# Clearing memory on another engine, and two moved transfers, in a fused gated-recurrence and squared-ReLU kernel

## The chip, the cores and the metric

The kernel runs on one core of a Trainium2 chip. A core has a matrix engine (TensorE, PE in the profile), an engine for elementwise work (VectorE, DVE), one for activation functions and copies (ScalarE, ACT), a programmable one (GpSimd, POOL) and one that mostly issues transfers (SyncE, SP). Each runs its own list of instructions in order, and they signal each other with semaphores. Transfers between the large memory and the on-chip memory are asked for from the queue of SyncE, ScalarE or GpSimd and are carried out by 16 DMA engines.

The metric is the time of one execution on the device in microseconds. Three runs of the kernel before the change gave 706.3 us as the median, 705.64 at the least and 706.55 at the most.

## The reference

A gated linear recurrence per head, and a feed-forward layer on its output. The shapes are 4 sequences, 8 heads, 768 steps, 48 channels a head; 3072 tokens, model width 384, inner width 2048.

```python
mag = sqrt(a_re**2 + a_im**2)
scale = minimum(mag, 0.999) / (mag + 1e-6)
a_re_n, a_im_n = a_re * scale, a_im * scale
for t in range(S):                              # S_re, S_im: [B, H, D, D], zero at first
    new_re = ar * S_re - ai * S_im              # ar, ai: a_re_n, a_im_n at step t
    new_im = ar * S_im + ai * S_re
    S_re, S_im = new_re + outer(k[t], v[t]), new_im
    y[t] = q[t] @ S_re
x = y as [B*S, H*D]                             # 3072 x 384
h = maximum(x @ w_in, 0)
out = (h * h) @ w_out                           # 3072 x 384
```

## The kernel before

The sequence is cut into chunks of 128 steps, and two chunks (`GC = 2`, `b` = 0 or 1) form a group; there are 12 groups (`NGR`). For each group VectorE and ScalarE make the operands (the gates, their running products, the scaled queries and keys), TensorE makes the attention-like products, and the token tile `x` goes through the feed-forward layer on TensorE.

The two weight matrices arrive as 64-bit words. They are fetched in 16 blocks, and VectorE decodes each with five instructions. The words of a block of `w_in` come in two halves of the partitions, one asked for from SyncE and one from GpSimd:

```python
def decode(dst, words, j):                      # dst: 128 x 768 elements of a weight matrix
    ...
    nc.vector.tensor_scalar(out=head, in0=high, scalar1=3, scalar2=0x3FFFFFF8, ...)       # L585
    nc.vector.scalar_tensor_tensor(out=head, in0=high, scalar=-2 ** 30, in1=head, ...)    # L587
    nc.vector.tensor_scalar(out=rest, in0=head, scalar1=-2 ** 23, scalar2=None, ...)      # L589
    ...
    nc.vector.scalar_tensor_tensor(out=rest, in0=low..., scalar=2.0 ** -52, in1=rest, ...) # L592
    tt(dst, head.bitcast(F32), rest, ALU.add)                                             # L480
```

The line L480 is a helper, `tt`, through which nearly all two-input operations of VectorE go. Some tiles have parts that no later instruction writes, or that are read before they are first written in full. They are cleared once:

```python
def turn_mask(step):
    if step == 0:
        nc.scalar.activation(out=sums[:, 0:1], in_=tiny, func=AF.Abs_reciprocal_sqrt)     # L538
        return
    if step == 2:
        for t in ([t[:, :, :, :, C:W] for t in qk_of] + last + [t[:, DM:] for t in vt]
                  + kt + prod + states[0] + states[1]):
            nc.gpsimd.memset(t, 0.0)                                                      # L544
        return
    ...
```

These are 16 instructions. Their sizes per partition, in 4-byte elements, are 2 x 48 (`qk`), 2 x 1040 (`last`), 4 x 16 (`vt`), 2 x 512 (`kt`), 2 x 24 (`prod`) and 4 x 512 (`state`). VectorE itself clears a few small tiles while the pools are set up, `carry` (288 elements, then 96 set to one) among them.

The steps of the operands that the text speaks of:

```python
def squares():                                   # o.0: ScalarE, L698
    nc.scalar.activation(out=tiles["sq"], in_=r[:, A_RE:A_IM + 1], func=AF.Square)
def sum_of_squares():                            # o.3: VectorE, L711, waits for the squares
    ...
def limit(): ...                                 # o.8, o.9: ScalarE, two copies of z (L683)
def lessened(): ...
def grown_factor(): ...                          # o.10: ScalarE, L743
def gates():                                     # o.11: VectorE
    ...                                          #   L749 (reads both copies)
    tt(both_parts, both_parts, f...)             #   L480
    ...                                          #   L753 (reads the factor)
def grown_squared():                             # o.22
    nc.gpsimd.memset(begun, 0.0)                 #   GpSimd, L763
    nc.scalar.activation(...)                    #   ScalarE, L764, then L766 and L767
def grow():                                      # o.13: VectorE, the scan L771
    ...
def last_heads():                                # o.21: SyncE, six transfers last<-qk, L831
    ...
```

Everything is ordered by hand. A long string names the steps, and each engine takes its part of each step in this order. The letters that matter here: `o` a step of the operands, `l` and `i` the loads of a group's inputs (`raw`), `f` and `j` the two halves of a fetch of words, `W` a check by ScalarE that reads a block's words, `D` the decoding of a block, `v` the load of a group's values (`vt`), `a` and `b` the steps of its two chunks, `g` the gap fill, `F` and `H` the first product and its squared ReLU, `Z` and `R` the products and sums of the second matrix, `s` a store, `M` the step `turn_mask`. Its beginning, one stretch around the first gap fill, and its end:

```python
"l0.0 M0 f0 j0 l0.1 i0.1 f1 j1 M2 f2 j2 v0 o0.0 o0.3 o0.1 o0.4 o0.5 o0.7 o0.2 M1 o0.8 "
"D0 o0.9 o0.10 o0.6 o0.11 W0 W1 D1 o0.22 f3 v1 j3 o0.12 W2 o0.13 o0.15 o0.14 f4 j4 W3 "
...
"v2 a0.7 o1.15 o1.14 g0 l2 i2 o1.16 F0.0 o1.17 F0.1 H0.0 D5 ..."
...
"Q11.2 Q11.1 Q11.0 Q11.3 Z11.3 R11.2 Z11.4 R11.3 Z11.5 R11.4 Z11.6 R11.5 s11.0 R11.6 "
"s11.1"
```

The gap fill copies parts of the token tile `x` into its unused partitions, and the first product of a group waits for it:

```python
def load_values(gi):                             # v
    for b, n in enumerate(groups[gi]):
        nc.sync.dma_start(out=vt[gi % 2 * GC + b][:, 0:DM], in_=in_turn(vtok, n))         # L520
def fill_gaps(i):                                # g
    for hh in range(HH):
        nc.sync.dma_start(out=x[pads(hh), 0:NG], in_=x[rows(hh), NG])                     # L955
def store(i, b):                                 # s
    nc.sync.dma_start(out=in_turn(out, groups[i][b]), in_=out_of[i, b])                   # L1002
```

The output tile of chunk 1 of a group, 128 x 384, is completed in two halves of columns (`left` is 0 to 191, `right` 192 to 383; `MH` = 192, `DM` = 384):

```python
elif r == 4:
    tt(o[1][:, right], chain, o[1][:, right], ALU.add)       # R.4, VectorE
elif r == 5:
    tt(o[0][:, right], others[1], o[0][:, right], ALU.add)   # R.5, VectorE
else:
    nc.scalar.copy(out=o[1][:, left], in_=chain)             # R.6, ScalarE, L1062
```

After the last store every engine reads `count`, a number that tells whether the data were in the ranges that this path is made for; with these data they are, and a general path (not shown) is jumped over.

Of the kernel before, what the change touches and what calls it, by code (L numbers as in the profile page):

```python
# [425 lines left out]
def quotient_path(ctx, tc, feat, vtok, w_in, w_out, w1, w2, out, n_seq, count):  # L426

    nc = tc.nc
    N, _, D, _, NP, C = feat.shape
    DM, FF = w_in.shape  # L430
# [4 lines left out]
    NGR = N // GC  # L435
# [34 lines left out]
    def pads(hh):  # L470
# [3 lines left out]
    groups = [[(bp * GC + b) * NCH + c for b in range(GC)]  # L474
              for bp in range(n_seq // GC) for c in range(NCH)]
# [37 lines left out]
    def in_turn(rows_, n):  # L513


        return rows_[n * C:(n + 1) * C].rearrange("(n j) m -> j n m", j=L)
# [18 lines left out]
# [6 lines that stand above are left out]

            for t in ([t[:, :, :, :, C:W] for t in qk_of] + last + [t[:, DM:] for t in vt]
                      + kt + prod + states[0] + states[1]):
                nc.gpsimd.memset(t, 0.0)  # L544
            return
        nc.scalar.copy(out=mask.rearrange("p (j n) -> p n j", j=L),
                       in_=plain.rearrange("p (n j) -> p n j", j=L))
        turned = pm.tile([C, C], F32, tag="m", name="turned")
        nc.tensor.transpose(turned, mask, ident)
        nc.scalar.copy(out=mask.rearrange("p (j n) -> p n j", j=L),  # L550
                       in_=turned.rearrange("p (n j) -> p n j", j=L))
# [398 lines left out]
    KH, MH = NFB // 2, DM // 2  # L950
# [44 lines left out]
    out_of = {}  # L995
# [3 lines left out]
        nc.scalar.copy(out=out_of[i, b], in_=o_of[i, b])  # L999

    def store(i, b):
        nc.sync.dma_start(out=in_turn(out, groups[i][b]), in_=out_of[i, b])  # L1002

# [36 lines left out]
    def outputs(i, r):  # L1042
# [27 lines left out]


    FRONT = (
        "l0.0 M0 f0 j0 l0.1 i0.1 f1 j1 M2 f2 j2 v0 o0.0 o0.3 o0.1 o0.4 o0.5 o0.7 o0.2 M1 o0.8 "
        "D0 o0.9 o0.10 o0.6 o0.11 W0 W1 D1 o0.22 f3 v1 j3 o0.12 W2 o0.13 o0.15 o0.14 f4 j4 W3 "
        "l1 i1 o0.16 W4 o0.17 D2 o0.18 o1.6 o0.19 f5 j5 o0.20 o1.0 W5 a0.1 o1.3 o0.21 o1.1 D3 "
        "a0.2 a0.3 o1.4 o1.5 a0.4 a0.8 o1.2 o1.7 f6 j6 b0.0 a0.9 o1.8 b0.1 b0.2 b0.5 o1.9 b0.6 "
        "D4 b0.3 b0.7 a0.0 b0.4 o1.10 W6 b0.8 o1.11 f7 j7 a0.5 o1.12 o1.22 a0.6 b0.9 o1.13 W7 "
        "v2 a0.7 o1.15 o1.14 g0 l2 i2 o1.16 F0.0 o1.17 F0.1 H0.0 D5 o1.18 F0.2 H0.1 o2.6 o1.19 "
        "f8 F0.3 H0.2 F0.4 H0.3 o1.20 o2.0 F0.5 H0.4 W8 a1.1 o2.3 o1.21 D6 a1.2 a1.3 o2.1 a1.4 "
        "a1.8 o2.4 o2.2 F0.6 D7 f9 H0.5 o2.5 a1.0 H0.6 a1.9 F0.7 a1.5 W9 f10 o2.7 a1.6 b1.1 "  # L1080
        "a1.7 D8 b1.0 o2.10 o2.8 H0.7 b1.5 o2.9 f11 b1.6 D9 b1.2 b1.3 b1.7 T0.0 b1.4 g1 W10 "
# [53 lines left out]
        "Z10.4 b11.5 b11.6 R10.4 Z10.5 b11.7 g11 Z10.6 R10.5 s10.0 F11.0 R10.6 s10.1 F11.4 "  # L1135
        "H11.0 F11.1 H11.4 X11.0 K0 Y11.0 F11.5 K1 H11.1 F11.2 H11.5 X11.1 Y11.1 F11.6 H11.2 "
        "F11.3 H11.6 X11.2 K2 Y11.2 F11.7 H11.3 Z11.0 H11.7 X11.3 Y11.3 Z11.1 R11.0 Z11.2 R11.1 "
        "Q11.2 Q11.1 Q11.0 Q11.3 Z11.3 R11.2 Z11.4 R11.3 Z11.5 R11.4 Z11.6 R11.5 s11.0 R11.6 "
        "s11.1")


    number_of = {}
# [1 line left out]
    def ranges(step):  # L1144
# [32 lines left out]
        "Z": half_product,  # L1177
        "R": outputs,
        "s": store,
        "f": fetch,  # L1180
        "j": lambda i: fetch(i, True),
# [4 lines left out]
        "l": load_parts,  # L1186
        "v": load_values,
        "M": turn_mask,
        "K": ranges,
    }  # L1190
# [13 lines left out]
@with_exitstack  # L1204
def kernel(
    ctx: ExitStack,
    tc: tile.TileContext,
    feat: bass.AP,
    vtok: bass.AP,
    w_in: bass.AP,  # L1210
    w_out: bass.AP,
    out: bass.AP,
    n_seq: int,
):
    nc = tc.nc
    DM, FF = w_in.shape
    wts = ctx.enter_context(tc.tile_pool(name="wts", bufs=1))
    w1 = wts.tile([P, DM // P, FF], F32, name="w1")
    w2 = wts.tile([P, FF // P, DM], F32, name="w2")
    count = wts.tile([1, 1], I32, name="count")  # L1220
    quotient_path(tc, feat, vtok, w_in, w_out, w1, w2, out, n_seq, count)
    n_good = nc.values_load(count, min_val=0, max_val=P)
    with tc.If(n_good < P):
        decode_weights(tc, w_in, w_out, w1, w2, feat.shape[2])
        general_path(tc, feat, vtok, w1, w2, out, n_seq)
# [30 lines left out]
```

## Time and profile before

| | us |
|---|---|
| median of three runs | 706.3 |
| span of the profiled execution, first to last instruction | 704.7 |
| TensorE busy | 623.7 (89%) |
| VectorE busy | 528.5 (75%) |
| ScalarE busy | 386.6 (55%) |
| GpSimd busy | 46.3 (7%) |

The mean granted TensorE clock is 0.996 of full speed. The busy shares are averages over stages with different limits: the first 200 us hold the decoding of the weights and the first groups, the rest the steady run. In 0 to 200 us VectorE is busy for 176.1 us and TensorE for 129.5; in 200 to 660 us TensorE is busy for 456.8 us of 460. A line of the timeline reads: start, duration, engine, source line, operation, the tile written and the tile read, their sizes, and in brackets how long the engine stood idle before and what released it. SPq, ACTq and POOL with DMA_DIRECT2D are issues of transfers. A line of the waits reads: the waiting engine, line and tile, what it waited for, and the total, the number of times and the longest.

### The profile page before, as it was taken

Reading aid. Unit: us, or ns where it says so; the run is one execution under the profiler, and the core shown is the slowest. Engines: PE = TensorE matmul, PEld = TensorE weight load, DVE = VectorE, ACT = ScalarE, POOL = GpSimd, SP = SyncE. Lnnn points to the kernel's source line nnn. Section 1 sums busy time; section 2 is a strip of 40 time slices with the busy share of each in tenths; the row PEclk is TensorE's granted clock in tenths of the full one; section 3 lists DMA queues with packets and bytes.
Section 4 is the critical chain, followed back from the end, with each engine's and each line's share of the span. In section 5 each row is a group of like instructions: output and inputs, shape, how many; then the busy total and the mean of one; then the engine's idle time right before and its main releaser. Section 6 shows DMA issues by size and latency. Waiting matters only on the chain.

```text
span 704.7 us, 12547 instructions
## 1 busy us (share of the span) xinstructions
PE 623.7 (89%) x4955; PEld 548.1 (78%) x4955; DVE 528.5 (75%) x916; ACT 386.6 (55%) x684; POOL 46.3 (7%) x106
## 2 busy tenths in 40 slices
PE   0007689999889999999999999999999999999995
PEld 0005577776578898998999989989989989989895
DVE  4998999999699786896785885995985976872130
ACT  6647487754648547537457557366376475340330
POOL 8322200000000000000000000000000000000000
PEclk9999999999999999999999999999999999999999
DMA  8776434461333063062061051151240340110101
GB/s 198 163 132 113 105 74 143 152 108 38 68 75 62 7 93 72 2 124 40 29 113 23 29 113 24 47 98 22 68 84 14 84 74 8 29 23 2 29 1 28
DMA packets 44036, 47.75 MB, mean 68 GB/s; under 512 B 6016, under 2 KB 38976, under 8 KB 43968
## 3 DMA queue, kind: packets, MB, share of 16 engines
q1 hardware_dynamic: 41280, 41.30, 28.0%
q0 software_dynamic: 2336, 5.21, 3.7%
q8 instruction: 41, 0.67, 0.4%
q10 hardware_dynamic: 352, 0.34, 0.2%
q14 instruction: 27, 0.22, 0.1%
HBM read 36.18 MB, written 4.72 MB: 58 GB/s over the span
## 4 chain that ended last, share of the span: by engine, by line
PE 73%; DVE 13%; DMA 7%; SPq 3%; ACT 2%; issue 1%; DVEq 0%; ACTq 0%
PE h_ps L961 30%; PE o_ps L1038 26%; PE a_ps L872 6%; DMA raw<-in_feat_dram 3%; PE y L898 3%; PE y L864 3%; PE add L919 2%; DVE ab L480 2%; PE tp L879 2%; DVE qk L480 1%; DMA words<-in_moe_w_in_dram 1%; SPq L831 1%; DMA vt<-in_vtok_dram 1%; DVE pr L480 1%; DVE room L480 1%
## 5 line engine op out<-in xcount | busy, mean ns | idle before, releaser
L961 PE MATMUL h_ps<-x,w 128*128 128x256 f32 x1152 | 257.6, 384 | 7.1 <-DMA x<-x 7.0
L961 PEld LDWEIGHTS h_ps<-x,w 128*128 128x128 f32 x1152 | 220.3, 192 | 38.5 <-issue 6.2
L966 ACT ACTIVATE h<-h_ps 128x512 f32<-128x512 f32 x96 | 57.5, 599 | 104.4 <-PE h_ps L961 96.0
L1038 PE MATMUL o_ps<-w,h 128*128 128x192 f32 x640 | 111.1, 328 | 0.0
L1038 PEld LDWEIGHTS o_ps<-w,h 128*128 128x128 f32 x640 | 103.6, 190 | 1.8 <-issue 0.9
L480 DVE TENSOR_TENSOR pr<-ab 128x384 f32<-128x384 f32 (+2 forms) x168 | 66.4, 413 | 4.4 <-ACT ab L757 0.5
L967 ACT ACTIVATE h<-h 128x512 f32<-128x512 f32 x96 | 60.6, 631 | 3.0
L879 PE MATMUL tp<-ident,qk 128*128 128x128 f32 x120 | 22.7, 301 | 43.2 <-DVE qk L480 41.3
L480 DVE TENSOR_TENSOR a<-a_ps,mask 128x1024 f32<-128x1024 f32 x24 | 29.4, 1223 | 39.7 <-PE a_ps L872 39.7
L480 DVE TENSOR_TENSOR mix<-h 128x256 f32<-128x256 f32 x40 | 16.9, 422 | 53.7 <-ACT h L967 53.7
L1038 PE MATMUL o_ps<-w_sum,mix 128*128 128x192 f32 x320 | 55.8, 328 | 0.0
L1038 PEld LDWEIGHTS o_ps<-w_sum,mix 128*128 128x128 f32 x320 | 52.0, 190 | 1.1 <-DVE state L480 0.7
L879 PEld LDWEIGHTS tp<-ident,qk 128*128 128x128 f32 x120 | 14.0, 148 | 49.5 <-issue 42.7
L480 DVE TENSOR_TENSOR ab<-pr 128x192 f32<-128x192 f32 (+1 forms) x180 | 45.8, 276 | 4.6
L480 DVE TENSOR_TENSOR qk<-ab,qk 128x768 f32<-128x768 f32 x48 | 44.9, 956 | 0.9
L683 ACT ACTIVATE qk<-raw 128x768 f32<-128x768 f32 x24 | 36.7, 1528 | 12.6 <-DVE raw L480 9.0
L977 PE MATMUL o_ps<-w,h 128*128 128x384 f32 x128 | 42.3, 488 | 0.0
L872 PE MATMUL a_ps<-qk 48*128 48x128 f32 x576 | 41.3, 293 | 0.0
L872 PEld LDWEIGHTS a_ps<-qk 48*128 48x128 f32 x576 | 36.5, 199 | 4.4 <-issue 4.3
L683 ACT ACTIVATE ab<-raw 128x768 f32<-128x768 f32 x24 | 37.1, 1564 | 2.3 <-DVE qk L480 2.3
L480 DVE TENSOR_TENSOR room<-ab,carry 128x1344 f32<-128x1344 f32 x24 | 36.3, 1552 | 2.2 <-ACT carry L800 2.2
L977 PEld LDWEIGHTS o_ps<-w,h 128*128 128x128 f32 x128 | 24.1, 190 | 16.2 <-DVE w L480 0.7
(106 smaller groups left out, 823.8 us busy)
## 6 DMA issues: line engine op xcount, KB each, us to landing
raw<-in_feat_dram SPq DMA_DIRECT2D x40, 288.0 KB
words<-in_moe_w_out_dram SPq DMA_DIRECT2D x8, 768.0 KB
last<-qk SPq DMA_DIRECT2D x72, 64.5 KB
vt<-in_vtok_dram SPq DMA_DIRECT2D x24, 192.0 KB
out_dram<-o SPq DMA_DIRECT2D x24, 192.0 KB
raw<-in_feat_dram SPq DMA_DIRECT2D x120, 32.0 KB
words<-in_moe_w_in_dram POOLq DMA_DIRECT2D x8, 192.0 KB, 6.5
words<-in_moe_w_in_dram SPq DMA_DIRECT2D x8, 192.0 KB
```

The costliest lines, as they stand in the source:

```text
L480: nc.vector.tensor_tensor(out=out, in0=in0, in1=in1, op=op)
L683: nc.scalar.activation(out=out.rearrange("p c j n -> p c n j"), func=AF.Copy, in_=in_.rearrange("p c (n j) -> p c n j", j=L), **kwargs)
L864: nc.tensor.matmul(ys[p_ % 2][crossed(hh, p_), p_ // 2], lhsT=states[b][1 - c_seq % 2][rows(hh), c, p_], rhs=operand(c, p_, rows(hh)), sta ...
L872: nc.tensor.matmul(ps[:, hh, p_], lhsT=operand(2 + c, p_, rows(hh)), rhs=operand(c, p_, rows(hh)), start=(c == RE), stop=(c == IM))
L879: nc.tensor.transpose(tp[:, g], operands[gi][:, 2 + c, b, g, 0:C], ident)
L898: nc.tensor.matmul(tiles["y"][p_ % 2][crossed(hh, p_), p_ // 2], lhsT=v[:, at:at + ROWS], rhs=tiles["am"][:, hh, p_], start=(first and p_ ...
L919: nc.tensor.matmul(add[rr, c, p_], lhsT=kt[c][:, p_, rr], rhs=v[:, at:at + D], start=True, stop=True)
L961: nc.tensor.matmul(ps[:, j], lhsT=w1[:, g, (2 * f + j) * P:(2 * f + j + 1) * P], rhs=x_of[i][:, g], start=(g == 0), stop=(g == NG - 1))
L966: nc.scalar.activation(out=h, in_=h_ps[i, f], func=AF.Relu)
L967: nc.scalar.activation(out=h, in_=h, func=AF.Square)
L977: nc.tensor.matmul(o_of[i, b], lhsT=tokens_of(i, f, b)[:, j], rhs=w2[:, k], start=(k == 0), stop=(k == NFB - 1))
L1038: nc.tensor.matmul(to, lhsT=x(k)[:, j], rhs=factor(z)[:, 2 * k + j], start=(z in (0, 1, 3) and k == j == 0), stop=(k == KH // 2 - 1 and j ...
```

## The change

It has three parts. The 16 memsets of `turn_mask` go from GpSimd to VectorE and, by the place of `M2` in the order, become its first work after the small tiles of the set-up; they are meant to be off GpSimd, whose queue also carries fetches, while VectorE has not begun yet. The very last output tile is stored in two halves of columns: the right half from SyncE as soon as it is complete (`s11.2`), the left one from ScalarE's queue behind its last copy (`s11.1`), so that less is left to store at the end. And the fetch of values `v2`, two transfers of SyncE, goes behind the gap fill `g0`, so that the gap fill does not stand behind it.

```diff
             for t in ([t[:, :, :, :, C:W] for t in qk_of] + last + [t[:, DM:] for t in vt]
                       + kt + prod + states[0] + states[1]):
-                nc.gpsimd.memset(t, 0.0)
+                nc.vector.memset(t, 0.0)
             return
...
     def store(i, b):
-        nc.sync.dma_start(out=in_turn(out, groups[i][b]), in_=out_of[i, b])
+
+        queue, cols = nc.sync, slice(0, DM)
+        if i == NGR - 1 and b:
+            queue, cols = (nc.scalar, slice(0, MH)) if b == 1 else (nc.sync, slice(MH, DM))
+        b = min(b, 1)
+        queue.dma_start(out=in_turn(out, groups[i][b])[:, :, cols], in_=out_of[i, b][:, cols])
...
     FRONT = (
-        "l0.0 M0 f0 j0 l0.1 i0.1 f1 j1 M2 f2 j2 v0 o0.0 o0.3 o0.1 o0.4 o0.5 o0.7 o0.2 M1 o0.8 "
+        "l0.0 M2 M0 f0 j0 l0.1 i0.1 f1 j1 f2 j2 v0 o0.0 o0.3 o0.1 o0.4 o0.5 o0.7 o0.2 M1 o0.8 "
...
-        "v2 a0.7 o1.15 o1.14 g0 l2 i2 o1.16 F0.0 o1.17 F0.1 H0.0 D5 o1.18 F0.2 H0.1 o2.6 o1.19 "
+        "a0.7 o1.15 o1.14 g0 v2 l2 i2 o1.16 F0.0 o1.17 F0.1 H0.0 D5 o1.18 F0.2 H0.1 o2.6 o1.19 "
...
-        "Q11.2 Q11.1 Q11.0 Q11.3 Z11.3 R11.2 Z11.4 R11.3 Z11.5 R11.4 Z11.6 R11.5 s11.0 R11.6 "
-        "s11.1")
+        "Q11.2 Q11.1 Q11.0 Q11.3 Z11.3 R11.2 Z11.4 R11.3 Z11.5 R11.4 s11.2 Z11.6 R11.5 s11.0 "
+        "R11.6 s11.1")
```

## The prediction, made before the changed kernel had run

> **What bounds the kernel now.** I read the busy slices first, then VectorE's waits, then the timeline of the one stretch that looked odd, then the end of the chain. The slices (tenths of 17.6 us each):
>
> ```profile
> PE   0007689999889999999999999999999999999995
> DVE  4998999999699786896785885995985976872130
> POOL 8322200000000000000000000000000000000000
> ```
>
> From about slice 11 on TensorE is full. Before it VectorE is, and GpSimd works in the first slice alone. So there are two regimes: up to about 205 us the set-up and decoding on VectorE lead, after that TensorE. VectorE's waits, the first answer for 0 to 30 us, the second for 30 to 205 us (total, times, longest):
>
> ```profile
> DVE room L711 <- ACT room L698: 7.2, 1, 7.2
> DVE room L480 <- ACT room L720: 2.1, 1, 2.1
> DVE ones L527 <- PEq L1247: 0.9, 1, 0.9
> ```
>
> ```profile
> DVE a L480 <- PE a_ps L872: 7.7, 4, 5.3
> DVE pr L480 <- POOL prod L925: 0.3, 1, 0.3
> ```
>
> After its start VectorE waits 8.0 us in 175, and not once for a DMA. The a_ps waits themselves hang on VectorE: TensorE waits there for `last`, a copy of VectorE's products. What is taken out of VectorE's work near 13 us should therefore move everything behind it. There the timeline shows (start, duration, engine, line, tile):
>
> ```profile
> 8.66 0.96 DVE L711 SCALAR_TENSOR_TENSOR room<-room 128x768 f32<-128x768 f32 x1 [7.16 <-ACT room L698]
> ...
> 13.04 1.89 POOL L544 MEMSET last<- 128x1040 f32 x2
> ...
> 13.57 4.87 DVE L585 TENSOR_SCALAR decoded<-words 128x768 int32<-128x768 int32 x1
> ...
> 16.08 1.94 POOL L544 MEMSET state<- 128x512 f32 x4
> ...
> 18.48 0.96 DVE L587 SCALAR_TENSOR_TENSOR decoded<-words,decoded 128x768 int32<-128x768 int32 x1
> ```
>
> The first instruction of the first decode takes 4.87 us. The uses of `words` give its kin:
>
> ```profile
> L585 DVE TENSOR_SCALAR decoded<-words x8: 550/556/4872, 13.6 to 106.4; 128x768 int32<-128x768 int32 x8
> ```
>
> Eight equal instructions, median 0.556 us, one of 4.872. It spans GpSimd's clearing (12.90 to 16.08 + 1.94 = 18.02 us) and ends at 18.44, 0.42 us after the last memset. A second pair says the same on a small scale:
>
> ```profile
> 107.98 0.22 POOL L925 TENSOR_SCALAR prod<-last 128x2 f32<-128x2 f32 x1
> 107.99 0.63 DVE L589 TENSOR_SCALAR decoded<-decoded 128x768 int32<-128x768 int32 x1
> ```
>
> GpSimd ends at 108.20, VectorE at 108.62: again 0.42 us later, with 0.63 in place of its usual 0.56. I read the 4.87 us as VectorE locked out by GpSimd.
>
> **What the Trainium skill says.** "SBUF — State Buffer", section "Who interferes with whom": VectorE in a two-port mode, which tensor_scalar can enter, and GpSimd share a pair of ports under an exclusive lock; whoever comes first keeps it and the other "fully blocks". The trace agrees: 768 integers in 0.56 us against 0.96 for the two-input form beside it, and the 4.87. The same section has an instruction with at most one SBUF input outside these modes free of it, so memsets on VectorE should not hold up GpSimd. "VectorE: DVE Perf Modes", section "Zero memsets can be issued as uint32 (trn2)", gives a memset one cycle per element; the trace has 0.30 us for 288 elements and 0.14 for 96, which is 0.83 ns per element and 0.06 us per instruction. "DMA: Bandwidth & Descriptors", section "Issuing engines are not separate DMA queues": a second queue saves only issue time. No comparison in this trace isolates that.
>
> **Part 1, the memory cleared by VectorE.** Off GpSimd go 16 memsets, 5.12 us (12.90 to 18.02). On VectorE they come right after `carry`, whose last memset starts at 1.36 us. Elements per partition: 2 x 48 + 2 x 1040 + 4 x 16 + 2 x 512 + 2 x 24 + 4 x 512 = 5360. At 0.83 ns that is 4.47 us, plus 16 x 0.06 = 0.96: 5.4 us, so VectorE is done near 6.9 us. Its first real work starts at 8.66, behind ScalarE's squares. The added work lies wholly in the 7.16 us wait and costs nothing.
> What goes is 4.87 - 0.56 = **4.3 us** of VectorE's time at 13.6. Does it survive? I moved the following steps forward by 4.3 us and looked for anything that does not move with them:
> - The first decode would end at 13.57 + 4.1 = 17.7 us (the third decode takes 42.20 to 46.34). The gates (L749) need ScalarE's two copies, done at 14.11 + 2.85 = 16.96: met. L753 near 20.3 needs the copy done at 17.60: met.
> - The second decode would start near 21.2 us in place of 25.47. ScalarE reads the same words from 20.85 on without a wait, so they have landed by then: met, with 0.4 us shown to spare.
> - The scan (L771), now at 29.51, would start near 25.2. ScalarE's steps ahead of it, 25.58 to 26.95 now, can begin when ScalarE is done with the words at 22.90, so end near 24.3: met by 0.9 us.
> - GpSimd's third fetch of words moves from 17.96 to about 12.9. It stands behind the second fetch on its own queue, so it can crowd only SyncE's loads. The DMA engines are full then (shares 0.9 to 1.0 from 8 to 24 us), but the words concerned are read near 25 us.
> - The next inputs (`raw`) are asked for at 33.82, after ScalarE's copy of the keys, so about 29.5; the DMA share at 30 to 36 us is 0.4 to 0.7, and there is room.
> From there each step waits for another step, none for a point in time. TensorE's full stretch begins 4.3 us earlier and keeps its length. I count 4.3.
>
> **Part 2, the last output in halves.** The end of the chain:
>
> ```profile
> 697.41 0.32 ACT L1062 COPY o<-o_ps 128x192 f32<-128x192 f32 x1 [7.48 <-PE o_ps L1038]
> 697.75 0.60 SPq L1002 DMA_DIRECT2D out_dram<-o  x1
> ```
>
> The span ends at 704.7, 6.9 us after that issue begins. By stretches of 0.4 us, the store's data move from about 698.9 to 701.1; 3.5 us of closing work follow, which nothing here touches. The right half of the last tile is final after VectorE's sum at 692.27 (0.36 us), so it can leave 5 us before the end; behind the last copy only 98 KB in place of 197 KB remain, in 128 rows of 768 bytes. If data time went with bytes, 2.2 us would become 1.1; if with rows, nothing would change. I take a third of the possible 1.1, **0.4 us**. The issue costs 0.6 us on either queue; ScalarE's own queue spares a signal of 0.02 us (697.73 to 697.75).
>
> **Part 3, one fetch behind the gaps.** Two issues of values (76.88, 1.35 us) stand ahead of the gap fill, issued at 78.34, though its tokens are ready at 77.66. The gap fill can go 0.7 us earlier. TensorE waits 5.8 us for it, and starts at 82.62. But the 72 matmuls it starts end at 101.2, and TensorE next stands for VectorE's products and, at 106.42, for decoded weights. **0 us**; the values are used much later.
>
> Sum: 4.3 + 0.4 + 0 = 4.7. 706.3 - 4.7 = 701.6; a few tenths may be lost at the second decode, so 701.7.
>
> **The rivals.**
> 1. The long instruction waits for late words, not for GpSimd; then nothing moves and the time stays near 706. For it: six transfers feed that decode. Against: earlier parts of that fetch had landed at 10.7 us, where GpSimd's next issue waited for them; the 0.42 us fits the clearing.
> 2. The loads become the front's bound. For it: the DMA engines are full from 8 to 24 us, and the second decode has only 0.4 us shown to spare. It would take back 1 to 2 us: 703 to 704.
> 3. TensorE's clock. It was granted 0.66 in 106 to 110 us, after a pause, and 12 matmuls took 3.98 us there against 2.60 later. "TensorE: Matmul & The Clock Gate", section "Part 1: The HAM clock gate (the "warmup" mystery)", has the window free-running, so a shifted start may meet it elsewhere: up to 1.4 us either way, mostly hidden behind VectorE.
> 4. The memsets outlast VectorE's wait. They would have to take over 7 us; each us beyond costs one.
>
> **Range and chances.** Rival 1 I give one in twenty, rival 2 one in five. Full gain with a good tail: 700.8; half the second decode's risk and no tail: 703.4. The gain is under 1%, so 2% is out of reach either way.
>
> **What would show it.** L585's first instance at 0.56 us and the longest of the eight near 0.56; 16 memsets on VectorE ending near 7 us; L771 first at 25.2; TensorE's last matmul ending 4.3 us sooner (697.37 to 693.1); last copy to the end of the span 7.0 to about 6.6 us. A wait of VectorE for words at 21 us would show rival 2; L585 still long, rival 1.

## The result and the profile after

| | before | after |
|---|---|---|
| median, us (range) | 706.12 (705.64 to 706.55) | 701.51 (701.23 to 701.99) |
| span of the profiled execution, us | 704.7 | 700.0 |
| VectorE busy, us | 528.5 | 529.2 |
| GpSimd busy, us | 46.3 | 42.1 |

The ratio is 0.9936, with a 95% interval of 0.9918 to 0.9953: 4.6 us less, inside 2%, and 0.2 us from the predicted 701.7. (The 706.12 is the median of four runs; the 706.3 that the prediction starts from is that of the first three.) But that the sum came out so close is luck in part: two of its terms were off in opposite directions, and most of what follows is about them.

The busy slices of the changed kernel (17.5 us each):

```profile
PE   0007779999889999999999999999999999999996
...
DVE  7998998999698886896785885995985976972120
...
POOL 6412200000000000000000000000000000000000
```

VectorE's first slice goes from 4 to 7 and GpSimd's from 8 to 6; the other digits of the three rows change by one at most. VectorE's waits for 0 to 30 us (total, times, longest):

```profile
DVE room L480 <- ACT room L720: 2.1, 1, 2.1
DVE room L711 <- ACT room L698: 1.3, 1, 1.3
DVE ones L527 <- PEq L1252: 0.9, 1, 0.9
```

The same view for 30 to 205 us:

```profile
DVE a L480 <- PE a_ps L872: 8.7, 4, 5.3
DVE pr L480 <- POOL prod L925: 0.3, 1, 0.3
```

The wait for ScalarE's squares has shrunk from 7.2 to 1.3 us; the memsets fill the rest of it. The waits behind 30 us have grown by 1.0 us, from 7.7 to 8.7 (a first hint of a loss). The timeline of 0 to 30 us (start, duration, engine, line, tiles):

```profile
1.46 0.16 DVE L544 MEMSET qk<- 128x48 f32 x2
...
1.78 0.93 DVE L544 MEMSET last<- 128x1040 f32 x1 [0.16 <-issue]
...
5.09 2.11 DVE L544 MEMSET state<- 128x512 f32 x4
...
8.52 0.96 DVE L711 SCALAR_TENSOR_TENSOR room<-room 128x768 f32<-128x768 f32 x1 [1.32 <-ACT room L698]
...
13.43 0.55 DVE L585 TENSOR_SCALAR decoded<-words 128x768 int32<-128x768 int32 x1
...
21.00 0.55 DVE L585 TENSOR_SCALAR decoded<-words 128x768 int32<-128x768 int32 x1
```

The uses of `words` up to 110 us again, the line of the first instruction of a decode (shortest, median, longest in ns, first and last start):

```profile
L585 DVE TENSOR_SCALAR decoded<-words x8: 549/552/561, 13.4 to 101.9; 128x768 int32<-128x768 int32 x8
```

The 16 memsets run from 1.46 to 7.20 us, inside the old wait. The first decode's first instruction takes 0.55 us in place of 4.87, and none of the eight is longer than 0.561. The second decode starts at 21.00 us without a wait. Up to here the prediction holds nearly to the digit.

To see how far the lead lives, I compare the starts of the scan (L771), which comes once for each group, and of the last copy:

| us | before | after | lead |
|---|---|---|---|
| first scan | 29.51 | 25.05 | 4.46 |
| second | 76.24 | 71.72 | 4.52 |
| third | 141.63 | 138.12 | 3.51 |
| fourth | 200.05 | 196.54 | 3.51 |
| fifth | 249.78 | 246.50 | 3.28 |
| last copy | 697.41 | 694.04 | 3.37 |
| end of the span | 704.7 | 700.0 | 4.7 |

The lead reaches the second scan whole, loses 1.0 us ahead of the third and 0.2 more by the fifth, and gets 1.4 us back behind the last copy. The place of the first loss in TensorE's timeline, kernel before:

```profile
104.76 1.51 PE L919 MATMUL add<-vt,kt 128*64 128x48 f32 x32 [1.38 <-ACT kt L884]
106.42 3.98 PE L961 MATMUL h_ps<-x,w 128*128 128x256 f32 x12
```

The same of the changed kernel:

```profile
100.24 1.95 PE L919 MATMUL add<-vt,kt 128*64 128x48 f32 x32 [1.38 <-ACT kt L884]
102.12 4.76 PE L961 MATMUL h_ps<-x,w 128*128 128x256 f32 x12
```

TensorE restarts behind its pause with 32 small products of L919 and then 12 of the first product. The table of windows gives the granted clock there (window, length, TensorE busy and its instructions, clock, DMA share, GB/s), first before:

```profile
98.50:102.00 3.50, 3.18 (x16) 1.00 0.00 0
102.00:105.50 3.50, 1.34 (x26) 0.97 0.49 73
105.50:109.00 3.50, 3.36 (x23) 0.54 0.84 203
```

And after:

```profile
98.50:102.00 3.50, 2.12 (x35) 0.60 0.64 96
102.00:105.50 3.50, 3.50 (x12) 0.50 0.98 308
105.50:109.00 3.50, 3.50 (x57) 0.93 0.94 342
```

Before, the clock is at half from 105.3 to 108.7 us, 3.4 us long; after, from 99.2 to 106.0, 6.8 us, twice that. So the 12 products, 3.98 us before, take 4.76 with the change; at full clock they take 2.86 (a run below). The L919 products ahead of them lose another 0.44. The change also has half clock at 201.6 to 205.0 us, where the kernel before has none; whether that is the 0.2 us lost by the fifth scan is not shown.

The end: last copy, then the issue of the store that follows it.

```profile
694.04 0.32 ACT L1067 COPY o<-o_ps 128x192 f32<-128x192 f32 x1 [7.48 <-PE o_ps L1043]
694.39 1.20 ACTq L1007 DMA_DIRECT2D out_dram<-o  x1
```

From the end of the last copy to the end of the span it is now 5.6 us; it was 7.0.

### The profile page after: what moved, and what is told of

Its sections match the earlier page's. It is cut to its first block, busy times and chain, and to the rows that moved or that the text cites. A ratio compares the mean times of both kernels' runs of the same rounds, so it can differ in the third digit from the quotient of the medians.

```text
span 700.0 us, 12544 instructions
## 1 busy us (share of the span) xinstructions
PE 623.4 (89%) x4955; PEld 547.2 (78%) x4955; DVE 529.2 (76%) x932; ACT 386.7 (55%) x684; POOL 42.1 (6%) x90
## 4 chain that ended last, share of the span: by engine, by line
PE 76%; DVE 13%; DMA 4%; SPq 2%; issue 2%; ACT 1%; POOL 0%; DVEq 0%; POOLq 0%
PE h_ps L961 32%; PE o_ps L1043 27%; PE a_ps L872 6%; PE y L898 3%; PE y L864 3%; DMA raw<-in_feat_dram 3%; PE add L919 2%; DVE ab L480 2%; PE tp L879 2%; DVE pr L480 2%; DVE room L480 1%; DMA words<-in_moe_w_in_dram 1%; PE o_ps L977 1%; DVE qk L480 1%; SPq L831 1%
## 5 line engine op out<-in xcount | busy, mean ns | idle before, releaser
L961 PE MATMUL h_ps<-x,w 128*128 128x256 f32 x1152 | 260.5, 386 | 6.9 <-ACT qk L683 4.7
L961 PEld LDWEIGHTS h_ps<-x,w 128*128 128x128 f32 x1152 | 222.1, 194 | 39.2 <-ACT qk L683 4.9
L480 DVE TENSOR_TENSOR pr<-ab 128x384 f32<-128x384 f32 (+2 forms) x168 | 66.4, 413 | 4.4 <-ACT ab L757 0.5
```

The costliest lines, as they stand in the source:

```text
L480: nc.vector.tensor_tensor(out=out, in0=in0, in1=in1, op=op)
L961: nc.tensor.matmul(ps[:, j], lhsT=w1[:, g, (2 * f + j) * P:(2 * f + j + 1) * P], rhs=x_of[i][:, g], start=(g == 0), stop=(g == NG - 1))
```

## The experiments

A ratio is to the kernel before on the same chip, with its 95% interval; "a lead" is that of the table above.

### Each part alone

```diff
 memsets_alone: the memsets and the place of M2 as in the change; stores and v2 as before
 store_alone:   store() and s11.2 as in the change; memsets and v2 as before
 fetch_alone:   "v2 a0.7 ... g0" becomes "a0.7 ... g0 v2"; all else as before
 memsets_and_store: the change without the moved v2
```

Expected of the memsets alone:

> Part 1 alone, on the kernel before. Main theory (GpSimd's clearing locked VectorE out for 4.3 us, and the front is VectorE's): the first L585 takes 0.56 us, the scan L771 starts 4.4 us earlier than before, and the time is 706.1 - 4.4 = 701.7 if all of it reaches the end, about 702.7 if 1 us is lost again to TensorE's clock around 100 us. Rival (most of the 4.6 us of the whole change came from the store and the fetch): 704 or more.

Of the store alone:

> Part 2 alone, on the kernel before. As the two profiles show it (6.97 us from the last copy to the end of the span before, 5.64 after): 1.3 us shorter, 704.8, with the last copy itself at the same time as before. As I predicted it: 0.4 us, 705.7. TensorE's last matmul ends at 697.4 as before in both.

Of the fetch alone:

> Part 3 alone, on the kernel before. Main theory: the first product starts 2 us earlier, TensorE then stands longer before the decoded weights, and the time stays at 706.1 +- 0.3. Rival (an earlier first product leaves TensorE idle for longer around 100 us, so its clock is lowered for 6.8 us in place of 3.4): 706.6 to 707.2, with the matmuls behind the pause at half clock for longer than before. Second rival (the earlier gap fill is worth something): below 705.6.

Of the first two together:

> The change without part 3. If the earlier first product cost 1 us by TensorE's clock: 700.4 to 700.7, 1 us better than the whole change, and the lead of the scan (4.5 us) still stands behind 110 us. If the clock is chance: as the whole change, 701.5, within 0.4.

| | median, us (range) | before | ratio | gain, us |
|---|---|---|---|---|
| memsets_alone | 703.44 (702.01 to 704.64) | 706.28 | 0.9956 [0.9939, 0.9972] | 2.8 |
| store_alone | 704.81 (703.55 to 706.67) | 706.28 | 0.9977 [0.9969, 0.9986] | 1.5 |
| fetch_alone | 706.52 (705.39 to 709.27) | 706.28 | 1.001 [0.9998, 1.0022] | -0.2 |
| memsets_and_store | 701.81 (700.74 to 702.94) | 706.28 | 0.9936 [0.9918, 0.9954] | 4.5 |

The gains of the three add up to 4.1, the whole change gives 4.6; within the intervals that is the same. The memsets are worth less than 4.3 (which is the very edge of the interval, 1.98 to 4.31 us) and less than either size put down for them (701.7 and 702.7), the halves more than 0.4 (interval 1.0 to 2.2 us), the fetch nothing. In fetch_alone the first product started at 80.06 in place of 82.62 us, 2.6 us sooner, of which 0.6 came from a shorter first decode in that run; the end did not follow, and the low clock there lasts 3.4 us as before. And memsets_alone and memsets_and_store show the same 6.8 us of low clock as the full change, at 99.3 to 106.2 and 98.2 to 105.0 us: the moved fetch does not cause it. How much it takes depends on where it falls: in memsets_and_store, 1 us earlier than in the change, the 12 products took 4.16 us and the lead fell by only 0.4 us, from 4.30 at the second scan to 3.93 at the third.

### Is it GpSimd's lock? Two memsets put back

```diff
-            for t in ([...] + last + [...]): nc.vector.memset(t, 0.0)
+            for t in ([...] + [...]): nc.vector.memset(t, 0.0)     # all but last
+    M3, behind j1:  for t in last: nc.gpsimd.memset(t, 0.0)        # 2 x 1040 elements
```

> The changed kernel, but GpSimd clears the two tiles of last (2 x 1040 elements, 1.89 us before) at the old place; VectorE clears the other fourteen. If the lock is the cause, L585's first instance ends 0.42 us after GpSimd's last memset: GpSimd begins at about 13.0, ends near 14.9, so L585 lasts 15.3 - 13.5 = 1.8 to 1.9 us, and the scan L771 comes 1.3 us later than in the changed kernel, 26.4. Rival (the long instruction waited for words): 0.56 us as in the changed kernel.

The timeline of this run, GpSimd's two memsets and the first decode's first instruction:

```profile
12.14 1.88 POOL L548 MEMSET last<- 128x1040 f32 x2
...
13.43 1.01 DVE L589 TENSOR_SCALAR decoded<-words 128x768 int32<-128x768 int32 x1
```

GpSimd started at 12.14 and not near 13, so the size that I had put down was missed: the instruction grew by 0.46 us and not by over a microsecond. The rule held to the hundredth: GpSimd ends at 14.02, the instruction at 14.44, 0.42 us later, as in both pairs of the kernel before. In all six traces with the 16 memsets on GpSimd it is 0.42. The first scan came at 25.51, 0.46 us later. The words of that decode were fetched as in the change, so late words do not explain it. What the Trainium skill says under "SBUF — State Buffer", section "Who interferes with whom", that the lock is held for the whole instruction, fits the 0.42 us, but not all: in the kernel before, 14 of GpSimd's 16 memsets were running or still to come when VectorE's instruction began, and it got in between none of them. The median time, 702.0 (ratio 0.9932 [0.991, 0.9953]), does not tell half a microsecond apart.

Six traces of kernels with the memsets on GpSimd show how much that instruction varies: 4.26, 4.29, 4.47, 4.53, 4.61 and 4.87 us. The one that I had predicted from was the longest; the mean is 4.50. What follows GpSimd's end is constant; how long the instruction takes depends on when GpSimd begins (12.31 to 13.03 us) and when VectorE arrives (13.28 to 14.10 us).

### Is the lost microsecond the clock? Spare products in TensorE's pauses

The edits add products whose result nobody reads, and leave everything else in place:

```diff
+    def spare_products(n):
+        ps = po.tile([P, DM], F32, tag="o", name="spare_ps")
+        for _ in range(n):
+            nc.tensor.matmul(ps[:, 0:P], lhsT=ident, rhs=ident, start=True, stop=True)
 spare_products: the change, "U4", "U3" and "U5" among the steps near 96 to 101 us (12 products)
 the *_kept_warm kernels: 13 more (U4 U2 U7) among those near 193 to 201 us
```

> The changed kernel with 12 spare 128x128 products of a constant on TensorE in its pause behind the sixth block of the first product (4, 3 and 5 of them, nobody reads them). If the lowered clock after that pause (6.8 us at 0.5) is what took 1 us of the lead: the clock stays at 1, the 12 matmuls behind the pause take 2.6 us in place of 4.8, the scan near 138 us comes 1 to 1.5 us sooner, and the time is 700.0 to 700.6. Rival (VectorE sets that stretch anyway): 701.5. If the spare products are too few to keep the clock up or hold up the real ones: 701.5 or more.

The 12 products behind the pause in this run:

```profile
102.59 2.86 PE L961 MATMUL h_ps<-x,w 128*128 128x256 f32 x12 [0.48 <-DVE w L480]
```

They take 2.86 us, and the bracket says that they now wait for VectorE, which decodes the weights. The lead at the third and fourth scan is 4.95 and 4.98 us: the loss ahead of the third is gone. But at 200.0 to 206.8 us the clock fell to half, for 6.8 us, and the last copy came at 695.20, a lead of 2.2; the median, 702.64 (0.9938 [0.9918, 0.9958]), shows no gain and misses the 700.0 to 700.6 expected. So I filled the second pause too, in three kernels: the change, the kernel before, and the memsets alone.

> The changed kernel with spare products of a constant in both pauses of TensorE, 12 around 96 to 101 us and 13 around 193 to 201 us. With 12 alone the scan near 195 us was 5.0 us ahead of before, but the clock was then lowered for 6.6 us at 200 us and the lead at TensorE's end fell to 2.2. If the clock is what takes the lead away: no lowered clock up to 210 us, a lead of about 5.0 at TensorE's end (692.4), and 699.5 to 700.3. If VectorE or the loads take it: 701.5 again.

> The kernel before with the same 25 spare products. If the clock is lowered there for one period of 3.4 us as a rule, keeping it up is worth 0.5 to 1 us: 705.3 to 705.9. If it is worth nothing there: 706.3.

> Part 1 alone with the same 25 spare products, to be held against before_kept_warm. If the 4.3 us of part 1 are right and only the clock took 1 to 1.5 of them in memsets_alone: 4.3 us less than before_kept_warm, 701.0 to 701.6. If the loss has another cause: 2.8 to 3.3 us less.

| | median, us (range) | ratio to before | third scan | last copy |
|---|---|---|---|---|
| changed_kept_warm | 700.49 (699.70 to 700.88) | 0.9911 [0.9897, 0.9926] | 136.20 | 692.11 |
| memsets_kept_warm | 701.79 (701.59 to 702.89) | 0.9933 [0.9920, 0.9946] | 136.12 | 692.68 |
| before_kept_warm | 705.30 (703.82 to 706.41) | 0.9982 [0.9974, 0.9990] | 139.45 | 695.38 |

The same windows as above, with the spare products in the change:

```profile
98.50:102.00 3.50, 2.80 (x45) 1.00 0.63 94
102.00:105.50 3.50, 3.40 (x34) 1.00 0.93 280
105.50:109.00 3.50, 3.50 (x57) 1.00 0.96 360
```

The clock stays up in both pauses. The third scan of the changed kernel comes 1.92 us sooner than without the spare products, the last copy 1.93, a lead of 5.3; the median is just above the 699.5 to 700.3 expected. The kernel before pays for the low clock too: its 12 products take 3.98 us where they could take 2.86. The plainest reading is the time from the second scan to the third. It is 65.39 us in the kernel before and 66.40 in the change, and the difference is the lost microsecond. With the spare products it is 64.29 in before_kept_warm, 64.28 in changed_kept_warm and 64.28 in memsets_kept_warm: the same, wherever the memsets are. So the clock is shown as the cause of this loss.

What that is worth in the whole time is less certain. In the medians the memsets are worth 705.30 - 701.79 = 3.5 us with the clock held, where they were worth 2.8 without; 3.5 lies inside the interval of the 2.8, and the expectation had been 4.3, or 2.8 to 3.3 if the loss had another cause. The two traces with spare products give less at the last copy: 695.38 - 692.68 = 2.7 us, where before and memsets_alone give 697.41 - 694.11 = 3.3. Of the lead of 4.0 us at the first scan 0.7 is lost at 60 us (below) and 0.6 behind the fourth scan, the latter without a cause found. The changed kernel with 25 spare products more is 1.0 us under the change in the medians (intervals overlap; 1.9 us in the traces) and 6.2 us under the 706.71 of the kernel before on the same chip.

Is the longer stretch of low clock a lasting effect of the shift, or luck? In the traces without spare products, the kernels with the memsets on GpSimd show one stretch of 3.4 us four times, and one of 6.8 us once (halves_on_sync); those with the memsets moved show one of 6.8 us three times, and in last_left_on_gpsimd two of 3.4 us, at 91.6 to 95.0 and 101.8 to 105.3 us. From the second scan to the third it takes 65.3 to 65.4 us in the first four, 65.8 in halves_on_sync, and 65.8 to 66.4 in those with the memsets moved. A longer stretch happens in both; whether the shift makes it likelier, nine traces do not settle. In all fourteen traces each recorded stretch of one clock within the run lasts a whole multiple of 3.41 us (3.41, 6.83, 10.24, 17.07 and so on), whatever the kernel does meanwhile.

### A third place: 60 us

The two first scans are 46.7 us apart in six of the seven runs so far with the memsets moved (47.1 in spare_products), but only 46.0 to 46.2 in three of six with them on GpSimd. The difference is VectorE's first wait for TensorE's `a_ps`. In the timeline of before_kept_warm:

```profile
63.12 0.61 PE L872 MATMUL a_ps<-last 48*128 48x128 f32 x8
...
63.78 1.23 DVE L480 TENSOR_TENSOR a<-a_ps,mask 128x1024 f32<-128x1024 f32 x1 [0.72 <-PE a_ps L872]
```

And of the change:

```profile
59.24 1.06 PE L872 MATMUL a_ps<-last 48*128 48x128 f32 x8
...
60.36 1.23 DVE L480 TENSOR_TENSOR a<-a_ps,mask 128x1024 f32<-128x1024 f32 x1 [1.44 <-PE a_ps L872]
```

Eight equal products take 0.61 us in one and 1.06 in the other, and VectorE waits 0.72 or 1.44 us. The clock column reads 1.00 for both, but there it says nothing: the trace's record of the clock begins at 62.8 us in the first and at 65.1 us in the second, and the time ahead of the record counts as 1.00. The products show that it was half until then. The kernel before, whose record begins at 88.2 us, shows it best: products of L961 start every 0.43 us up to 87.9 us and every 0.22 from 88.3 us on. (So the mean clocks of 0.996 and the like leave these first stretches out.) For the lead it means this: memsets_kept_warm is 4.04 us ahead of before_kept_warm at the first scan and 3.31 at the second, 0.73 less, and its wait is 1.4 us. In all seven traces before the next run with the memsets moved, which come here some 4 us sooner, the wait was 1.43 or 1.44 us. To raise the rate, 36 spare products on the third decode's weights, from 42 us on, were added to changed_kept_warm:

```diff
-"... D2 o0.18 ..."
+"... D2 U36 o0.18 ..."     # rhs = w1[:, 0, 2 * BLK:2 * BLK + P] in place of ident
```

> The changed kernel with the 25 spare products of changed_kept_warm and 36 more behind the third decode, near 42 to 50 us, where TensorE stands idle ahead of its first products. In every trace with the memsets on VectorE the first 24 a_ps products (near 56.5 us) took 2.93 us and VectorE waited 1.44 us for a_ps; in three of six traces with the memsets on GpSimd, where everything comes 4 us later, the last of them already ran at the full rate (8 products in 0.61 in place of 1.06 us) and the wait was 0.7 to 0.9 us. Theory (TensorE is still at half speed there because it has stood idle, and this is a second place where the lead of part 1 is lost): 24 products 1.61 us, VectorE's wait for a_ps under 0.7 us, the second scan 45.3 to 46.0 us behind the first in place of 46.7, and 0.7 to 1.4 us less than changed_kept_warm: 699.1 to 699.8. Rival (the half speed near 60 us is no matter of idleness, or the wait is for something else): 2.93 and 1.44 us as before, 46.7 us between the scans, 700.5.

TensorE's timeline in this run:

```profile
42.41 9.67 PE L1153 MATMUL spare_ps<-w,ident 128*128 128x128 f32 x72 [28.16 <-DVE w L480]
51.91 0.49 PE L879 MATMUL tp<-ident,qk 128*128 128x128 f32 x3
...
57.17 2.93 PE L872 MATMUL a_ps<-qk 48*128 48x128 f32 x24
59.89 1.06 PE L872 MATMUL a_ps<-last 48*128 48x128 f32 x8
```

A miss. The spare products did raise the rate (three transpositions, 0.49 us at 51.91; 0.87 in the change), but between 52.4 and 55.4 us TensorE stands idle for 2.4 us, and at 57.17 it was slow again (the record has the clock at half from 55.5 us on): 2.93 us, VectorE's wait 1.6 us, 46.8 us between the scans. The time, 699.89 (699.47 to 701.99; 0.9913 [0.9896, 0.9930]), is that of changed_kept_warm within the intervals. That this 0.7 us can be had is not shown.

### Why is the end worth more? The store taken apart

```diff
 whole_store_on_scalar: queue = nc.scalar if i == NGR - 1 and b else nc.sync    # whole tile
 halves_on_sync: as in the change, but (nc.sync, slice(0, MH)) for the last half
```

> The kernel before with the last tile stored whole, but from ScalarE's queue. From the last copy to the end of the span is 7.0 to 7.3 us where SyncE stores it whole and 5.6 to 6.0 where the left half goes by ScalarE. If the queue does it: 5.6 to 6.0 here too, and 704.8. If the halved bytes do it: 7.0 to 7.3, 706.3.

> The kernel before with the last tile in halves, both from SyncE. If the halved bytes do it: 5.6 to 6.0 us from the last copy to the end, 704.8. If the queue does it: 7.0 to 7.3, 706.3. If each does a part: between.

| | ratio to before | end of the last copy to the end of the span, us |
|---|---|---|
| whole tile, SyncE (five traces) | 1 | 7.0 to 7.5 |
| halves, both SyncE | 0.9986 [0.9975, 0.9997] | 6.3 |
| whole tile, ScalarE | 0.9982 [0.9974, 0.9991] | 6.1 |
| halves, SyncE and ScalarE (ratio of store_alone; seven traces) | 0.9977 [0.9969, 0.9986] | 5.5 to 5.9 |

The three intervals overlap, so by the times alone the variants cannot be put in order. The traces say more, though there is only one for each of the two middle rows: the whole 197 KB sent from ScalarE's queue give 0.9 to 1.4 us, and halving on top of it 0.2 to 0.6; halving without another queue gives 0.7 to 1.2. Either does a good part of it, so it is not a matter of bytes alone. Nor is it issue time, to which the prediction had held a second queue: the issue itself took longer on ScalarE, 1.20 us against 0.60. After its last work each engine reads `count`, branches over the general path (COMPARE_BRANCH), and its next instruction (EVENT_SEMAPHORE) comes microseconds later. The uses of that line, near the end, kernel before (columns: shortest, median, longest in ns, first and last start):

```profile
L1223 SPq EVENT_SEMAPHORE  x8: 17/17/17, 702.5 to 703.0; - x8
...
L1223 ACTq COMPARE_BRANCH  x1: 54/54/54, 698.0 to 698.0; - x1
...
L1223 SPq COMPARE_BRANCH  x1: 45/45/45, 698.4 to 698.4; - x1
...
L1223 ACTq EVENT_SEMAPHORE  x1: 17/17/17, 701.1 to 701.1; - x1
```

And of the changed kernel, where it is line 1228:

```profile
L1228 SPq EVENT_SEMAPHORE  x8: 17/17/17, 696.6 to 697.4; - x8
...
L1228 SPq COMPARE_BRANCH  x1: 45/45/45, 692.5 to 692.5; - x1
...
L1228 ACTq COMPARE_BRANCH  x1: 54/54/54, 696.4 to 696.4; - x1
L1228 ACTq EVENT_SEMAPHORE  x1: 17/17/17, 699.0 to 699.0; - x1
```

Before, SyncE issues the last store, branches at 698.4 and comes back at 702.5, 4.1 us later. The span ends 2.2 us after that. After, SyncE has branched at 692.5, ahead of the last copy, and is back at 696.6; now ScalarE comes last, from 696.4 to 699.0, and the span ends 1.0 us behind it. This holds in all fourteen traces: where SyncE branches last, the end is 2.2 us behind its return (six traces, before, memsets_alone, fetch_alone and halves_on_sync among them); where ScalarE does, 1.0 us behind ScalarE's (eight, after, store_alone and whole_store_on_scalar among them). Why does a branch of 45 ns cost 4 us? The DMA view of the kernel before, from 701.8 to 702.4 us:

```profile
q14 instruction: 1, 0.01, 3.2%
```

It shows one transfer, of instructions, and no store data, which ended by 701.0. That agrees with the Trainium skill, "Runtime: NRT & Kernel Launch", section "Instruction fetch mechanics": a taken branch whose target lies outside the fetched stretch has the engine wait for a transfer of the target page. But it does not prove it: here the transfer ends at 702.27, 0.2 us before SyncE's return, while in the five other traces where SyncE branches last the last such transfer to end before the return does so 0.8 to 1.5 us ahead of it. What the traces do show is that the store's data have landed before SyncE is back, so that the return and not the data ends the chain. With half the data behind the last copy and both halves from SyncE, the return took 3.3 us and not 4.0 to 4.5 as in the thirteen other traces: the bytes act, it seems, by holding up that return, but one trace is too little to say so. Taking the branch away was not tried, so why the return takes microseconds stays open.

## Why the prediction was right, and where only in sum

- **Part 1, the lock.** Right in its mechanism and its places: memsets hidden, ending at 7.20 (predicted near 7), L585 at 0.55, first scan at 25.05 (predicted 25.2), `raw` asked for at 29.37 (29.5), no wait at the second decode. Rivals 1, 2 and 4 are out: the long instruction was not late words, no load became VectorE's bound (ScalarE's wait for words near 31 us grew from 0.55 to 1.75 us, and the lead at the second scan was still whole), and 1.3 us of VectorE's wait were left.
- **Part 1, "From there each step waits for another step, none for a point in time ... I count 4.3."** This step failed. TensorE's rate does hang on a point in time. At the last copy, which waits for TensorE's last matmul, 3.37 us were left and not 4.3. This is rival 3, which I had bounded well (1.4 us either way) and then put away with "mostly hidden behind VectorE". At 102 us it was not hidden: with the clock held, the 12 products took 1.9 us less and the third scan came 1.92 us sooner, and between the second scan and the third nothing of the lead was lost. A second, smaller term is the size of the lock itself, read from one trace: 4.87 us, where the mean of six is 4.50, so about 3.9 us to be had and not 4.3.
- **Part 2.** The term that was mis-sized the other way: 0.4 predicted, 1.4 in the traces of before and after, 1.5 alone. I had reasoned on how long the store's data take, and called what follows "3.5 us of closing work ..., which nothing here touches". The change touches it: SyncE branches at 692.5 in place of 698.4 us, ahead of the last copy, and the closing work had hung on SyncE's return. That the issue costs 0.6 us on either queue was wrong too: it cost 1.20 on ScalarE's.
- **Part 3.** 0 predicted; -0.2 us in the medians, -1.6 to 0.1 by the ratio's interval, for the reason given: TensorE's first products end ahead of VectorE's in any case. Only the shift was mis-sized: they started 2.0 us sooner and not 0.7.
- **The sum.** In the traces, 3.4 + 1.4 = 4.7 (3.37 + 1.36 unrounded) in place of 4.3 + 0.4 = 4.7. That the two errors are of one size is luck.

## What to carry to other kernels

Where one instruction is almost nine times as long as its kin and ends a fixed bit after another engine's work, find that work and move it into a wait that is there anyway. A lead won early is only kept if nothing on the way hangs on a point in time, as TensorE's clock did here; compare the starts of one instruction that recurs, group by group, and see where the lead shrinks. At the end of a program ask which engine issues last and what it still has to do after that, not only how many bytes it stores.

## What was unexpected in the hardware

- An engine that jumps over code came back microseconds after the branch (SyncE 3.3 to 4.5 us, ScalarE 2.5 to 3.5, in fourteen traces).
- The same store issue took 1.20 us on ScalarE and 0.60 on SyncE; ScalarE's queue still gave the earlier end.
- 25 products whose result nobody reads made the kernel before faster, 0.9982 [0.9974, 0.9990], 1.4 us, by holding the clock up.
- TensorE ran at half its later rate near 60 us, where the trace has no record of the clock yet and the column reads 1.00; the spacing of equal products (0.43 against 0.22 us) changes just where the record begins.
